# Batch 2's plain attention pairs computed in 64x64 quadrants, in three visits instead of two

## The chip, the cores and the metric

The kernel runs on one core of a Trainium2 chip. The metric is the device time of one execution in microseconds (us). The kernel before takes 300.69 us, the median of three runs (300.37 to 300.76). The engines are PE (TensorE, matrix multiply; PEld is its weight load), DVE (VectorE), ACT (ScalarE), POOL (GpSimd, which here mostly issues DMAs) and SP (SyncE, which issues DMAs). Each engine takes its own instructions strictly in the order in which the program wrote them, and waits on semaphores for the others.

## The reference

```
# q, k, v: 8 batches, 8 heads, 576 tokens, 64 dims; D = 64
mask_plain = (rel >= 0) & (rel < 32)                       # heads 0 to 3
mask_dil = (rel >= 0) & (rel < 128) & (rel % 4 == 0)       # heads 4 to 7
scores = where(mask, q @ k.T / sqrt(D), -1e9)
attn = exp(scores - max); attn /= sum(attn) + 1e-9
x = (attn @ v) reshaped to 4608 tokens x 512
h = maximum(x @ w_in, 0)                                   # 512 x 2048
out = (h * h) @ w_out                                      # 2048 x 512
```

So it is a banded attention, with half of the heads plain (the last 32 tokens) and half dilated (every fourth of the last 128), and then a two-layer network with a squared relu.

## The kernel before, in words

**The two layers set the pace.** The 4,608 tokens go through the layers in tiles: four of 256 tokens (they start at tokens 0, 256, 512, 768) and then seven of 512. A tile's work is cut into groups of a few matmuls, numbered from 0: first-layer groups (`mm1` in `ffn_groups`, line 905; the result goes through ACT's relu, L918, and DVE's square, L919) and second-layer groups (`g2`, line 947, four matmuls of 512 columns each; after four groups the output is copied to SBUF by ACT, L953, and stored by SP). The tile at token 768 has groups 48 to 63 (in order: 48 and 49 with the first three k-tiles, 50 and 51 with the last one, 52 to 55 whole, 56 to 63 second-layer); the tile at token 1024 starts at group 64. The tuple `kts` is the order in which a first-layer group takes its four k-tiles; k-tile e is the part of x that pair e of heads has written.

**Attention is put between the groups.** Heads go in pairs: pairs 0 and 1 are plain, 2 and 3 dilated. Work for a batch is a list of small steps, and a hand-written schedule says after which group each is emitted. There are two schedules: `PROGRAM`, a string whose parts between bars belong to groups -1, 0, 1, ..., and the list `steps` at the end of the kernel, of (group, rank within it, batch, code). Nothing reorders them later: the order of emission is the order on each engine.

A code of `PROGRAM` has batch, kind, pair and home: `2q1` and `2k1` turn pair 1's q and k of batch 2 by PE transposes (L258) and copy them from PSUM into `qT` (L278) and `kbd` (L282); who copies q follows `copier`: ACT for plain pairs, or DVE where the code ends in `v`. `2k1l` and `2k1h` do the two heads separately. `2a0` and `2b0` are the first and second part of pair 0's scores over the whole 128x128 array (L332), with ACT's exp (L342) and DVE's mask (L343). `2o0` and `2p0` are the products with v (L395) and the sums with ones (L397), with ACT's Ln and Exp (L399, L400) that make the reciprocal, and DVE's multiply into `xT` (L410). `1b3` and `1p3` are the same for batch 1. A pair's two heads share one 128-row operand there, with zeros in the other half (`kbd` and `vbd` hold block diagonals).

A code of `steps` that begins with V is a **visit**: the function `quadrants` takes scores of some pairs and products of others and issues them as 64x64 matmuls (L629), each on one of four quadrants of the array, which run side by side; the quadrant is (row half g, column half c). `V022,23/` is batch 2's scores of pairs 2 and 3. R00, R01, R10 and R11 (`arrange`, L479 and L482, on DVE) copy the end blocks of the dilated q and k for row half g (first digit) from the tile `xx` into `kbd`; a visit's dilated scores read both. E20 and E21 are the exp (ACT, L666) and mask (DVE, L668) of pair 2's two halves. L2 is the Ln of the sums (L642, L643), X2 the reciprocal's Exp (L652) and the multiply into `xT` (DVE, L655, L657). A plain pair in a visit also has two additions on DVE that its sums share (L680).

In the kernel before, batch 2 (`XB`) is mixed. Its dilated pairs go through visits: the scores after group 56, the products after group 59 together with batch 3's first scores (pair 2). Its plain pairs go through `PROGRAM`, over the whole array, between groups 39 and 56. Batches from 3 on are in quadrants throughout. The accumulators of a visit are PSUM tiles of four pools: `pa` (two buffers), `pf` (four), `po` and `pd` (one each); a visit waits until the buffers that it takes over have been read.

Of the kernel before, what the change touches and what calls it, by code (L numbers as in the profile page):

```python
# [12 lines left out]
RES = 4  # L13
# [12 lines left out]
    "X21 M21 L31 X31 M31 E01 E11 | L2:q00123 L2:q10123 L1:v1dpr | | P01 D01 L01 X01 M01 P11 D11 L11 X11 M11 | | | "  # L26
    "| | | | | | | | | m n | | | | | | 1q1 1q3 | 1q2f 1k2f | 1k1a 1v3 | 1a2 | 1v2 1k0a 1q0v | 1o2 | 1a0 1a1 | 1k3 "
    "1o0 1o1f | 1a3 1Q0 | 1K0 1o3 | 1Q1 1K1 | 1Q2 | 1b0 | | 1Q3 1K2 L2:vwp L3:q00123 L3:q10123 L2:vwdr | L2:x f | "
    "| 2q0 | | 2k0 1V2 | 1b2 1p0 | 1b1 1V3 1K3 | L3:x | 1p2 1p1f | 2a0 1b3 | 2k1l 2b0 2o0 1p3f 2k1h | 2q1 | | 2p0 "
    "L3:Vd0 L4:q00123 L4:q10123 L3:V1 2a1 | 2b1 | | 2o1 | | | 2p1f | | | | L4:x | | | | | | | | | | | | | | | | | "  # L30
    "| L4:Vd L5:q10123 L5:q00123 L4:V01 | | | | | | | | | | | | | | | | L5:x | L5:Vd L6:q10123 L6:q00123 L5:V01"
)


# [29 lines left out]
def kernel(  # L64
# [9 lines left out]
    nc = tc.nc  # L74
# [99 lines left out]

    def crossed(b: int, e: int):

        return int(b == XB and e == 3 or b >= NATURAL and e == 1 or b >= PAIRED and e == 0)

    def load_v(b: int, parts, which="pdr"):


        dst = vbd[b % 2]
        if b not in vds:
            vds[b] = vd_pool.tile([P, NE // 2, 2, RES * D], bf16, name="vd")
        p0, p1 = parts[0], parts[-1] + 1
        i0, i1 = 4 * p0, 4 if p1 == 1 else NB
        sides = [(hl, slice(64 * hl, 64 * hl + 64)) for hl in range(2)]
        for what in which:
            if what == "p":
                for e in range(NE // 2):  # L190
                    for hl, rows in sides:
                        nc.gpsimd.dma_start(  # L192
                            dst[rows, e, i0:i1, rows],
                            v[b, 2 * e + hl, 64 * i0 : 64 * i1, :].rearrange("(i p) d -> p i d", p=64),
                        )
            elif what == "d" and len(parts) == 1:
                for hl, rows in sides:
                    nc.gpsimd.dma_start(  # L198
                        vds[b][rows, :, p0, :],
                        v[b, H // 2 + hl : H : 2, 256 * p0 : 256 * p1, :].rearrange("e (p r) d -> p e (r d)", r=RES),  # L200
                    )
            elif what in "d01":
                for e in (0, 1) if what == "d" else (int(what),):
                    for hl, rows in sides[::-1] if crossed(b, e + NE // 2) else sides:
                        hl = hl ^ crossed(b, e + NE // 2)
                        nc.gpsimd.dma_start(
                            vds[b][rows, e, :, :],
                            v[b, H // 2 + 2 * e + hl, 0:512, :].rearrange("(m p r) d -> p m (r d)", p=64, r=RES),
                        )
            elif b == XB:  # L210
                for g, rows in sides:
                    for i in (0, 8):
                        nc.gpsimd.dma_start(
                            dst[rows, NE // 2 : NE, i, rows],
                            v[b, H // 2 + g : H - g : 3 - 2 * g, 64 * i : 64 * i + 64, :].rearrange("h p d -> p h d"),
                        )
            elif p1 == 2:
                for hl, rows in sides:
                    nc.gpsimd.dma_start(
                        dst[rows, NE // 2 : NE, 8, rows],  # L220
                        v[b, H // 2 + hl : H : 2, 512:S, :].rearrange("h p d -> p h d"),
                    )
# [271 lines left out]
    def quadrants(scs, pvs):  # L494
# [14 lines left out]
        for n, (b, e) in enumerate(pvs):  # L509
# [2 lines left out]
            o, d = (pool.tile([P, 512], f32, name=name) for pool, name in pools)  # L512
            if double:
                to = main_s[crossed(b, e)]
                rest = [to[:, 448:512]] * 2, [to[:, 384:448]] * 2
            else:
                rest = ([t[:, 448:512] for t in main_s],) * 2
# [64 lines left out]
        for n, (b, e) in enumerate(scs):  # L582
            ps = extra if n else main_s
            sp[b, e] = ps
            dil = e >= NE // 2
            swap = double and n == 0
            if swap:
                turned.add((b, e))
            for g, c in todo:
                items = scored[n][g, c]  # L590
                rows, h = sides[g], 2 * e + (c ^ crossed(b, e))
                to = ps[g ^ c if swap else g]
                for z in range(4):
                    if dil:
                        x, y = z % 2, 80 * z
                        lhs = kx[b % 2][rows, h, z // 2, 64 * x : 64 * x + 64]
                        rhs = qx[b % 2][rows, h, z // 2, 16 + 48 * x : 96 + 48 * x]
                        out, cols = to[:, y : y + 80], 80
                    else:
                        i = 2 * z + g  # L600
                        lhs, rhs = k_both[rows, i, h, :], q_both[rows, h, :, 16 * i : 16 * i + 24]
                        out, cols = byr(to[:, 96 * z : 96 * z + 96]), 96
                    items.append(("s", out[sides[c]], lhs, rhs, cols))
                if dil:
                    hd = h - H // 2
                    lhs, rhs, y = ends[b % 2][rows, 1, hd, :], byr(ends[b % 2][rows, 0, hd, :]), 320
                elif g == 0:
                    lhs, rhs, y = k_both[rows, 8, h, :], q_both[rows, h, :, 128:M], 384
                if dil or g == 0:
                    items.append(("s", byr(to[:, y : y + 64])[sides[c]], lhs, rhs, 64))  # L610
# [20 lines left out]
    def natural_step(b: int, code: str):  # L631
# [28 lines left out]
        else:  # L660
# [3 lines left out]
            n = 384 if e >= NE // 2 else (448, 384)[g]  # L664
            pt = pts[b, e][:, 448 * g : 448 * g + n]
            nc.scalar.activation(pt, sp[b, e][g][:, 0:n], ACT.Exp, scale=SCALE)  # L666
            mask = (mask_f if e >= NE // 2 else mask_n)[:, 0:n]
            nc.vector.tensor_tensor(out=pt, in0=pt, in1=mask, op=ALU.mult)  # L668
            if g and e >= NE // 2 and b > XB:
                z = pts[b, e][:, :].rearrange("p (x y) -> p x y", x=2)[:, :, 0:320].rearrange("p x (c m) -> p x c m", c=2)  # L670
# [206 lines left out]
    def ffn_groups(tk0: int, nt: int):  # L877
# [3 lines left out]
        early = NT <= tk0 <= 3 * NT  # L881
        h2 = h2_pool.tile([P, NF, NT], bf16, name="h2T")
        per = NT // nt
        kts = (2, 0, 3, 1) if tk0 > 3 * NT else (2, 3, 0, 1) if tk0 == 3 * NT else (0, 2, 1, 3) if NT <= tk0 < 2 * NT else (0, 1, 2, 3) if tk0 in (0, 2 * NT) else (2, 3, 0, 1)
        cut = 3 if tk0 >= NT and tk0 != 2 * NT else 2
        cur, acc = {}, {}

# [51 lines left out]
        def g2(m, part):  # L939
            last = tk0 + P * (m + 1) == NTOK  # L940
            if part == 0 or last and part == 2:
                cur[m] = ps_f.tile([P, DM], f32, name="pf")

            c0, c1 = ((0, 384), (384, DM))[part // 2] if last else (0, DM)
            f0, f1 = (NF // 2 * (part % 2), NF // 2 * (part % 2 + 1)) if last else (4 * part, 4 * part + 4)
            for f in range(f0, f1):
                nc.tensor.matmul(  # L947
                    cur[m][:, c0:c1], h2[:, f, P * m : P * m + P], w_out_sb[:, f, c0:c1],
                    start=(f == 0), stop=(f == NF - 1),
                )  # L950
            if f1 == NF:
                osb = osb_pool.tile([P, DM], f32, name="osb")
                (nc.vector.tensor_copy if last and part == 1 else nc.scalar.copy)(osb[:, c0:c1], cur[m][:, c0:c1])  # L953
                pos = tk0 + (P * m + half) % nt if over else tk0 + P * m
                for x in (c0, DM // 2) if c1 - c0 == DM and tk0 == NTOK - NT else (c0,):
                    store(osb, pos, x, DM // 2 if x < c0 + DM // 2 and c1 - c0 == DM and tk0 == NTOK - NT else c1)
# [123 lines left out]
    groups[:NF] = [head[y] for y in (0, 1, 2, 3, 16, 4, 5, 17, 18, 19, 20, 21, 6, 7, 22, 23)]  # L1080
    groups[NF:G] = [head[y] for y in (8, 9, 12, 13, 10, 11, 14, 15)] + head[24:32]
    for x, code in enumerate(("R00", "R01", "R10", "R11")):
        steps.append((48 + x, 1, XB, code))
    steps.append((56, 2, XB, "V022,23/"))
    steps += [(57, 1, XB, f"E{e}{x}") for e in (2, 3) for x in range(2)]
    for b in range(NATURAL, B):
        t = G * (b - 1)
        early = b == NATURAL
        def visit(at, scs, pvs):
            steps.append((at, 2, b, "V0" + "/".join(",".join(f"{x}{y}" for x, y in z) for z in (scs, pvs))))  # L1090

        def expo(e, *at):
            steps.extend((y, 1, b, f"E{e}{x}") for x, y in enumerate(at))
# [3 lines left out]

        after = b + 1 < B
        if b < PAIRED:
            start = 59 if early else t - 8  # L1100
            second = t + (7 if early else 5)
            x = 3 if early else 0
            if early:
                visit(start, [(b, 2)], [(XB, 2), (XB, 3)])
                for e in (2, 3):
                    steps.extend([(start + e - 2, 3, XB, f"L{e}"), (start + e - 1, 0, XB, f"X{e}")])
            expo(2, *((start + 4, start + 7) if early else (start + 7, start + 9)))
            visit(second, [(b, x)], [(b, 2)])
            norm(2, second)
            expo(x, second + 3, second + 5)  # L1110
# [81 lines left out]
```

## Time and profile before

| | |
|---|---|
| median of three runs | 300.69 us |
| the profiled execution | 300.98 us |
| its span, first to last instruction | 299.2 us |
| PE busy | 290.3 us, 97% |
| ACT busy | 195.2 us, 65% |
| DVE busy | 168.3 us, 56% |
| POOL busy | 129.4 us, 43% |

The profile is of one execution. Busy is the time in which at least one instruction of the engine ran. The span is cut into 40 slices of 7.5 us for the rows of digits, where 9 means 90% or more; the row PEclk is the granted TensorE clock in tenths. The chain of waits follows back from the last instruction to what released each, and gives shares of the span by engine. A timeline row has start, duration, engine, line, operation, output and inputs, shapes and a count; instructions overlap, so that the distance between starts tells more than the sum of durations.

Around the change, batch 2's work stands between 60 and 88 us: the first dilated scores begin at 80.57, the visit with the dilated products at 83.74, and the tile at token 1024 begins at 88.19.

### The profile page before, as it was taken

Reading aid. Unit: us, or ns where it says so; the run is one execution under the profiler, and the core shown is the slowest. Engines: PE = TensorE matmul, PEld = TensorE weight load, DVE = VectorE, ACT = ScalarE, POOL = GpSimd, SP = SyncE. Lnnn points to the kernel's source line nnn. Section 1 sums busy time; section 2 is a strip of 40 time slices with the busy share of each in tenths; the row PEclk is TensorE's granted clock in tenths of the full one; section 3 lists DMA queues with packets and bytes.
Section 4 is the critical chain, followed back from the end, with each engine's and each line's share of the span. In section 5 each row is a group of like instructions: output and inputs, shape, how many; then the busy total and the mean of one; then the engine's idle time right before and its main releaser. Section 6 shows DMA issues by size and latency. Waiting matters only on the chain.

```text
span 299.2 us, 7686 instructions
## 1 busy us (share of the span) xinstructions
PE 290.3 (97%) x3056; PEld 168.3 (56%) x3085; DVE 168.3 (56%) x503; ACT 195.2 (65%) x407; POOL 129.4 (43%) x210
## 2 busy tenths in 40 slices
PE   8989999999999999999999999999999999999994
PEld 3589756968855454554455455545554455445443
DVE  1676556997858764687749564866455234004300
ACT  6788658859967765788667666767666567127411
POOL 8589873484695475955792689000000000000000
PEclk9999999999999999999999999999999999999999
DMA  7999999999999989989999499012101200121022
GB/s 105 196 167 214 207 144 234 191 160 191 173 127 184 184 106 201 151 127 174 157 202 145 59 166 186 8 30 70 45 0 28 82 35 2 35 71 35 2 70 70
DMA packets 83123, 35.42 MB, mean 118 GB/s; under 512 B 52624, under 2 KB 78480, under 8 KB 83088
## 3 DMA queue, kind: packets, MB, share of 16 engines
q0 software_dynamic: 49280, 18.43, 54.7%
q1 hardware_dynamic: 33120, 16.18, 25.5%
q8 instruction: 24, 0.39, 0.5%
q10 hardware_dynamic: 688, 0.33, 0.5%
q14 instruction: 11, 0.09, 0.1%
HBM read 37.40 MB, written 9.44 MB: 157 GB/s over the span
## 4 chain that ended last, share of the span: by engine, by line
PE 89%; DMA 5%; POOL 3%; issue 1%; ACT 0%; DVE 0%; ACTq 0%; POOLq 0%
PE pf L947 41%; PE pf L905 40%; DMA w_in<-in_moe_w_in_dram 5%; PE po L629 2%; PE pa L258 1%; PE pa L629 1%; PE pf L629 1%; POOL vbd L192 1%; PE pd L629 1%; POOL qb L171 1%; POOL kb L171 1%; PE pa L332 1%; PE po L395 1%; PE pd L397 0%; POOL vd L198 0%
## 5 line engine op out<-in xcount | busy, mean ns | idle before, releaser
L905 PE MATMUL pf<-xT,w_in 128*128 128x512 bf16 (+1 forms) x697 | 128.2, 340 | 1.0 <-DMA w_in<-in_moe_w_in_dram 0.6
L947 PE MATMUL pf<-w_out_sb,h2T 128*128 128x512 bf16 (+2 forms) x570 | 127.4, 373 | 1.5 <-issue 0.6
L905 PEld LDWEIGHTS <-w_in 128*128 128x128 bf16 x704 | 77.8, 113 | 46.9 <-DMA w_in<-in_moe_w_in_dram 0.9
L918 ACT ACTIVATE h2T<-pf 128x512 bf16<-128x512 f32 x144 | 83.6, 599 | 30.0 <-PE pf L905 29.8
L919 DVE TENSOR_TENSOR h2T<-h2T 128x512 bf16<-128x512 bf16 x144 | 60.3, 425 | 60.2 <-ACT h2T L918 57.9
L947 PEld LDWEIGHTS <-h2T 128*128 128x128 bf16 x592 | 55.4, 98 | 61.2
L953 ACT COPY osb<-pf 128x512 f32<-128x512 f32 (+1 forms) x36 | 20.7, 575 | 51.1 <-PE pf L947 47.1
L457 POOL DMA_DIRECT2D vbd<-in_v_dram x80 | 43.4, 552 | 20.8 <-DMA kb<-in_k_dram 8.1
L171 POOL DMA_DIRECT2D qb<-in_q_dram x18 | 13.0, 720 | 12.8 <-DMA xx<-qb 9.2
L652 ACT ACTIVATE rec<-rec 128x576 f32<-128x576 f32 x22 | 15.0, 682 | 0.6
L192 POOL DMA_DIRECT2D vbd<-in_v_dram x16 | 10.9, 688 | 9.5 <-DMA kb<-in_k_dram 2.6
L666 ACT ACTIVATE pt<-pa 128x384 bf16<-128x384 f32 (+1 forms) x26 | 11.8, 495 | 4.5 <-DVE xT L657 2.7
L655 DVE TENSOR_TENSOR xT<-po,rec 128x512 bf16<-128x512 f32 x13 | 9.0, 692 | 8.8 <-ACT rec L652 8.5
L444 POOL DMA_DIRECT2D vd<-in_v_dram x20 | 12.1, 617 | 3.7 <-DMA vbd<-in_v_dram 2.0
L171 POOL DMA_DIRECT2D kb<-in_k_dram x18 | 12.7, 705 | 0.3 <-issue 0.2
L449 POOL DMA_DIRECT2D vbd<-in_v_dram x20 | 12.2, 631 | 0.9 <-DMA vbd<-in_v_dram 0.7
L668 DVE TENSOR_TENSOR pt<-pt,mask_n 128x448 bf16<-128x448 bf16 (+1 forms) x20 | 7.1, 373 | 9.4 <-ACT pt L666 9.3
L668 DVE TENSOR_TENSOR pt<-pt,mask_f 128x384 bf16<-128x384 bf16 x24 | 8.3, 355 | 5.8 <-ACT pt L666 5.8
L471 DVE COPY qT<-xx 64x576 bf16<-64x576 bf16 (+1 forms) x30 | 10.7, 358 | 0.6
L655 DVE TENSOR_TENSOR xT<-pf,rec 128x512 bf16<-128x512 f32 x9 | 6.2, 692 | 7.1 <-ACT rec L652 7.1
L629 PEld LDWEIGHTS <-vbd 64*64 64x64 bf16 x248 | 6.8, 107 | 3.8 <-issue 3.3
L473 DVE COPY kbd<-xx 64x320 bf16<-64x320 bf16 (+3 forms) x32 | 8.2, 256 | 0.6
(140 smaller groups left out, 323.2 us busy)
## 6 DMA issues: line engine op xcount, KB each, us to landing
qb<-in_q_dram POOLq DMA_DIRECT2D x7, 320.0 KB, 7.1
kb<-in_k_dram POOLq DMA_DIRECT2D x7, 320.0 KB, 8.1
vd<-in_v_dram POOLq DMA_DIRECT2D x32, 64.0 KB, 6.1
w_in<-in_moe_w_in_dram POOLq DMA_DIRECT2D x4, 512.0 KB, 7.7
w_out_sb<-in_moe_w_out_dram POOLq DMA_DIRECT2D x4, 512.0 KB, 12.7
out_dram<-osb SPq DMA_DIRECT2D x16, 128.0 KB, 4.3
qb<-in_q_dram POOLq DMA_DIRECT2D x7, 256.0 KB, 7.4
kb<-in_k_dram POOLq DMA_DIRECT2D x7, 256.0 KB, 7.6
```

The source lines that it names most:

```text
L171: nc.gpsimd.dma_start(t[0:n, part, hs, :], src[b, hs, t0 : t0 + RES * n, :].rearrange("h (p r) d -> p h (r d)", r=RES))
L192: nc.gpsimd.dma_start(dst[rows, e, i0:i1, rows], v[b, 2 * e + hl, 64 * i0 : 64 * i1, :].rearrange("(i p) d -> p i d", p=64),)
L457: nc.gpsimd.dma_start(v_rows[b % 2][p0 + 16 * r : p0 + 16 * r + 16, e, :, :], v[b, 2 * e + hl, :, :].rearrange("(i m r) d -> r m i d", r=R ...
L629: nc.tensor.matmul(out, lhs, rhs, start=begin, stop=True, skip_group_check=True)
L652: nc.scalar.activation(rec[:, :], rec[:, :], ACT.Exp, scale=-1.0)
L655: nc.vector.tensor_tensor(out=tok[:, :, 16:M], in0=byr(o[:, :]), in1=byr(rec[:, 0:512]), op=ALU.mult)
L668: nc.vector.tensor_tensor(out=pt, in0=pt, in1=mask, op=ALU.mult)
L905: nc.tensor.matmul(to, w_in_sb[piece][:, kt, c0 : c0 + 509 : 4], rhs, start=(kt == kts[0] and x == 0), stop=(kt == kts[-1] and x == per - ...
L918: nc.scalar.activation(hv, acc[u][:, :].rearrange("p (x n) -> p x n", x=per), ACT.Relu)
L919: nc.vector.tensor_tensor(out=hv, in0=hv, in1=hv, op=ALU.mult)
L947: nc.tensor.matmul(cur[m][:, c0:c1], h2[:, f, P * m : P * m + P], w_out_sb[:, f, c0:c1], start=(f == 0), stop=(f == NF - 1),)
L953: (nc.vector.tensor_copy if last and part == 1 else nc.scalar.copy)(osb[:, c0:c1], cur[m][:, c0:c1])
```

## The change

Batch 2's plain pairs go through visits too.

- `PROGRAM` loses 2a0, 2b0, 2o0, 2p0 and 2a1, 2b1, 2o1, 2p1. 2q1 becomes 2q1v: DVE copies the q of pair 1 instead of ACT.
- The visit with the dilated scores moves from after group 56 to after group 50; R00 to R11 go from groups 48, 49, 50, 51 to 48, 49, 49, 50. A second visit after group 55 has the plain scores and the dilated products. A third, after group 61 (it was after 59), has the plain products and batch 3's first scores.
- `quadrants` learns batch 2's plain scores: each head's nine blocks lie in one quadrant, pair 0 on (0,0) and (1,1), pair 1 on (0,1) and (1,0). For that, pair 1 is `crossed`: its v blocks are loaded with the two heads in the opposite halves.
- The mask of these pairs is a part of `mask_p` instead of `mask_n`. The spare columns for the end blocks come from another tile where a visit has two of each kind.
- The tile at token 1024 takes its k-tiles in the order 2, 3, 0, 1 instead of 0, 1, 2, 3. The two output copies of the tile at token 768 go from ACT to DVE.

```diff
-    "| 2q0 | | 2k0 1V2 | 1b2 1p0 | 1b1 1V3 1K3 | L3:x | 1p2 1p1f | 2a0 1b3 | 2k1l 2b0 2o0 1p3f 2k1h | 2q1 | | 2p0 "
-    "L3:Vd0 L4:q00123 L4:q10123 L3:V1 2a1 | 2b1 | | 2o1 | | | 2p1f | | | | L4:x | | | | | | | | | | | | | | | | | "
+    "| 2q0 | | 2k0 1V2 | 1b2 1p0 | 1b1 1V3 1K3 | L3:x | 1p2 1p1f | 1b3 | 2k1l 1p3f 2k1h | 2q1v | | L3:Vd0 "
+    "L4:q00123 L4:q10123 L3:V1 | | | | | | | | | | L4:x | | | | | | | | | | | | | | | | | | L4:Vd L5:q10123 "
...
-        return int(b == XB and e == 3 or b >= NATURAL and e == 1 or b >= PAIRED and e == 0)
+        return int(b == XB and e in (1, 3) or b >= NATURAL and e == 1 or b >= PAIRED and e == 0)
...
-                            v[b, 2 * e + hl, 64 * i0 : 64 * i1, :].rearrange("(i p) d -> p i d", p=64),
+                            v[b, 2 * e + (hl ^ crossed(b, e)), 64 * i0 : 64 * i1, :].rearrange("(i p) d -> p i d", p=64),
...
                 to = main_s[crossed(b, e)]
+                if full and scs[0][1] < NE // 2:
+                    to = (extra if n else main_s)[1]
...
-            swap = double and n == 0
+            swap = double and n == 0 and dil
...
+                if b == XB and not dil:
+                    for i in range(NB) if c == g ^ crossed(b, e) else ():
+                        z, y = 96 if i < 8 else 64, 96 * (i // 2)
+                        out = byr(ps[i % 2][sides[c], y : y + z])
+                        rows = sides[g]
+                        items.append(
+                            ("s", out, kbd[rows, e, i, rows], qT[rows, e, :, 16 * i : 16 * i + z // RES], z)
+                        )
+                    continue
...
-            mask = (mask_f if e >= NE // 2 else mask_n)[:, 0:n]
+            mask = (mask_f if e >= NE // 2 else mask_p[:, 384:] if b == XB else mask_n)[:, 0:n]
...
-        kts = (2, 0, 3, 1) if tk0 > 3 * NT else (2, 3, 0, 1) if tk0 == 3 * NT else (0, 2, 1, 3) if NT <= tk0 < 2 * NT else (0, 1, 2, 3) if tk0 in (0, 2 * NT) else (2, 3, 0, 1)
+        kts = (2, 0, 3, 1) if tk0 > 3 * NT else (2, 3, 0, 1) if tk0 in (2 * NT, 3 * NT) else (0, 2, 1, 3) if NT <= tk0 < 2 * NT else (0, 1, 2, 3) if tk0 == 0 else (2, 3, 0, 1)
...
-                (nc.vector.tensor_copy if last and part == 1 else nc.scalar.copy)(osb[:, c0:c1], cur[m][:, c0:c1])
+                (nc.vector.tensor_copy if last and part == 1 or tk0 == 3 * NT // 2 else nc.scalar.copy)(osb[:, c0:c1], cur[m][:, c0:c1])
...
-        steps.append((48 + x, 1, XB, code))
-    steps.append((56, 2, XB, "V022,23/"))
-    steps += [(57, 1, XB, f"E{e}{x}") for e in (2, 3) for x in range(2)]
+        steps.append(((48, 49, 49, 50)[x], 1, XB, code))
+    steps.append((50, 2, XB, "V022,23/"))
+    steps += [(50 + e - 2 + x, 3, XB, f"E{e}{x}") for e in (2, 3) for x in range(2)]
+    steps.append((55, 2, XB, "V020,21/22,23"))
+    steps += [(55, 3, XB, "E10"), (55, 3, XB, "E11"), (55, 3, XB, "L3"), (56, 0, XB, "X3")]
+    steps += [(56, 1, XB, "E00"), (56, 1, XB, "E01"), (57, 3, XB, "L2"), (58, 0, XB, "X2")]
...
-            start = 59 if early else t - 8
+            start = 61 if early else t - 8
...
-                visit(start, [(b, 2)], [(XB, 2), (XB, 3)])
-                for e in (2, 3):
-                    steps.extend([(start + e - 2, 3, XB, f"L{e}"), (start + e - 1, 0, XB, f"X{e}")])
-            expo(2, *((start + 4, start + 7) if early else (start + 7, start + 9)))
+                visit(start, [(b, 2)], [(XB, 0), (XB, 1)])
+                for y, e in enumerate((1, 0)):
+                    steps.extend([(start + y, 3, XB, f"L{e}"), (start + y + 1, 0, XB, f"X{e}")])
+            expo(2, *((start + 3, start + 6) if early else (start + 7, start + 9)))
```

Lines of the changed kernel are 11 higher than those named here from about line 660 to 1080.

## The prediction

> **What bounds the kernel now.** I read the page first: its busy table and its chain of waits.
>
> ```profile
> PE 290.3 (97%) x3056; PEld 168.3 (56%) x3085; DVE 168.3 (56%) x503; ACT 195.2 (65%) x407; POOL 129.4 (43%) x210
> ...
> PEclk9999999999999999999999999999999999999999
> ...
> PE 89%; DMA 5%; POOL 3%; issue 1%; ACT 0%; DVE 0%; ACTq 0%; POOLq 0%
> ```
>
> TensorE (PE) is busy 97% of the span, at full granted clock, and holds 89% of the chain; DVE and ACT hold 0%. After the first weights land (24.5 us) PE never rests for long. So the sum is simple: the end moves by the PE time that is taken out, plus every new wait that PE takes on.
>
> Next I read PE's timeline where batch 2's plain pairs stand now. Columns: start, us, engine, line, operation, tiles, shape, count. The time of a piece is the distance to the start of the next piece (the second column has the pipeline's tail in it).
>
> ```profile
> 68.11 0.32 PE L332 MATMUL pa<-qT,kbd 128*128 128x96 bf16 x4
> 68.27 0.41 PE L338 MATMUL pa<-qT,kbd 128*128 128x32 bf16 x8
> ...
> 69.69 0.39 PE L332 MATMUL pa<-qT,kbd 128*128 128x32 bf16 x6
> 69.92 0.32 PE L395 MATMUL po<-pt,vbd 128*128 128x96 bf16 x4
> 70.07 0.32 PE L397 MATMUL pd<-pt,mk 128*128 128x96 bf16 x4
> 70.23 0.44 PE L395 MATMUL pf<-pt,vbd 128*128 128x32 bf16 x9
> ...
> 72.04 0.45 PE L258 MATMUL pa<-mk,qb 80*128 80x80 bf16 x8
> 72.32 1.91 PE L905 MATMUL pf<-xT,w_in 128*128 128x256 bf16 x16
> 74.08 0.39 PE L395 MATMUL po<-pt,vbd 128*128 128x32 bf16 x6
> 74.30 0.39 PE L397 MATMUL pd<-pt,mk 128*128 128x32 bf16 x6
> 74.52 0.32 PE L332 MATMUL pa<-qT,kbd 128*128 128x96 bf16 x4
> ```
>
> Pair 0's pieces are scores 0.16 (68.11) and 0.23 (69.69), products 0.31 (69.92 to 70.23) and 0.44 (74.08 to 74.52): 1.14 us; the two pairs 2.28.
>
> Last I read DVE's timeline, because the visit that the change pulls forward lives on what DVE writes.
>
> ```profile
> 69.98 0.98 DVE L282 COPY kbd<-pa 64x288 bf16<-64x288 bf16 x2
> ...
> 73.81 0.19 DVE L479 COPY kbd<-xx 64x128 bf16<-64x128 bf16 x1
> 73.92 0.30 DVE L482 COPY kbd<-xx 64x128 bf16<-64x128 bf16 x1
> 74.23 0.19 DVE L479 COPY kbd<-xx 64x128 bf16<-64x128 bf16 x1
> ...
> 78.44 0.19 DVE L479 COPY kbd<-xx 64x128 bf16<-64x128 bf16 x1
> ```
>
> L479 with L482 is one step R (end blocks of q and k): 0.42 us. The fourth, R11, runs at 78.44; the visit that reads it begins at 80.57. Today it has 2 us to spare.
>
> **PE work, part by part.** Out: the plain pieces, 2.28, and the two old visits, 0.70 (80.57 to the next GEMM at 81.27) and 1.21 (83.74 to 84.95): 4.19. In: three visits. Group 50's (dilated scores) holds the same 40 matmuls as the old one: 0.70. Group 55's has per quadrant 1,536 columns of dilated products and 832 of plain scores, 2,368; the nearest row is the visit of 108 matmuls and up to 2,272 columns at 141.45 to 142.64, 1.19, which scaled by columns is 1.24. Group 61's has 1,440 columns of plain products and 384 of batch 3's scores, 1,824, the same form as the visit at 111.61 to 112.83: 1.22. Together 3.16. **Net -1.03 us**. Taken alone that would be the gain.
>
> **What loses its cover.** I take the before trace's clock up to 68.11 and follow the built order of the changed kernel, with durations of these rows.
>
> PE: 1b3's scores 68.11 to 68.39, four GEMMs (0.86) to 69.25, the k transposes to 69.54. The products 1p3 come next, with no 2b0 and 2o0 in between. They need 1b3's mask: ACT's previous Exp ends 68.77, the exp of 512 (0.59) about 69.3, DVE's mask (0.43) 69.76. PE waits 0.26, and does the products (0.49) until 70.29. Then 12 GEMMs (1.31), q transposes (0.29), 12 GEMMs (1.31), 4 GEMMs (0.44): at **73.64** PE arrives at group 50's visit. Some 320 columns in, at 73.8, its last end blocks need R11.
>
> DVE, strictly in its order: two L282 after the mask, 0.98, to 70.7; the L410 multiply of 1p3, whose Ln and Exp put it 1.17 us behind the sums (66.80 to 67.97 in an earlier step), at 71.46 to 71.87; two more L282 to 72.9; then the four copies of 2q1, which ACT did until now; R00, R01, R10, 1.26; two squares L919 (0.76 for two), which stand ahead of R11; R11, 0.42.
>
> The four q copies (64x288, from PSUM, on DVE) are not in the trace. Below: the same line on DVE at 64x160 (58.31 to 59.34, four in 1.03) gives 1.03. Above: L282 at 64x288, about 0.49 each, 1.96. I take 1.30, 0.325 each, from the growth of that line from 64x128 (222 ns) to 64x160 (239 ns). So R11 ends at 72.9 + 1.30 + 1.26 + 0.76 + 0.42 = 76.6. PE is released at about 76.7: **a new wait of 2.9 us**, in three pieces (PSUM buffer of the q copies, R01, R11). Queued behind it on PE is everything: the GEMMs, whose relus feed ACT.
>
> [...]
>
> Even a faster DVE leaves a floor. The squares wait for two relus of the last four GEMMs: the first starts about 73.6, the two take 1.08 (ACT's pair at 74.16), a square 0.42, R11 0.42: 75.5. The wait is at least 1.7.
>
> Behind it things are tight but nearly covered. Between the visits of groups 55 and 61 stand 24 GEMMs, 5.2 us; ACT has exps, logarithms and reciprocals of 4.6 and DVE a multiply of 0.9 behind them, overlapping by some 0.5: 0 to 0.3 of wait. After group 61's visit PE has eight GEMMs, then eight with the k-tiles 2 and 3 that the new order puts first, 3.46 us; the last multiply of today's visit ends 3.35 after the visit (88.29 against 84.95). I put 0.2 on both; without the new k-tile order it would be 1.7 more.
>
> At nothing: exp, mask, sums and normalisation of the plain pairs (ACT gives up 5.4 us and takes 5.1; DVE gives up 3.3 and takes 4.1, some 0.8 more) run under GEMMs. The two output copies moved from ACT (0.58 each) to DVE aren't shown in that shape; DVE's 128x384 copy is 0.56 and its 128x512 multiply from PSUM 0.69, so I take 0.69. Both run under the GEMMs between visits 55 and 64; if that cover went, the last multiply, and PE, would be up to 0.7 late. The v loads swap halves, with as many DMAs; SP's and POOL's orders stay. The q and k transposes that group 50 reads landed by 62.2, the dilated v of group 55 by 77.9, before either is wanted.
>
> **Sum.** -1.03 + 0.26 + 2.9 + 0.2 - 0.1 (a wait before the visit at 80.57 that goes) = +2.2 us. The profiled run took 300.98 (span 299.2, 1.8 around it), 0.29 above the median 300.69; on the median this is **302.9**.
>
> **Rivals.**
> 1. *The visit does not wait* (faster): if R11 were done when PE comes, at 73.8, -1.03 + 0.26 - 0.1 = -0.9 stays, 299.8. For it: DVE is busy only 56%, and R has 2 us of slack today. Against: the visit moves from 80.57 to 73.64, 6.9 us forward, and R11 with it only by as much as DVE's queue lets it; R11 would have to end 2.8 us sooner, and it stands behind squares that PE's own last GEMMs release. The change is a gain where this wait stays below 0.7 (0.9 less the 0.2 at the later visits). Chance 0.10.
> 2. *DVE is quicker than I think, ACT's relus set the wait*: the floor, 1.7, with no waits later: +0.6 to +1.4, 301.3 to 302.1. For it: DVE is idle 0.7 before the multiply at 71.46. Chance 0.16.
> 3. *More is late*: copies at 0.49 (+0.7), 0.5 more at groups 55, 61 and 64, together 304.1; I give it 303.7 to 304.6. Chance 0.12. PEclk is 9 throughout today, so no row shows what a PE that stands for 2.9 us does to the granted clock. [...]
> 4. *The quadrants bring less*: if the plain pairs' two diagonals did not run side by side, the visits at 55 and 61 cost the 832 + 1,440 columns again, 0.95, and the gain goes: about 303.9, in case 3's range. Against it: the 111.61 row, the same form. Chance 0.03.
> The forecast, 302.1 to 303.7, keeps 0.59.
>
> **Numbers.** A measurement of this kernel tells about 0.2% (0.6 us) from no change. Faster by more: 0.10. Within: 0.05 (the low end of case 2, and a wait of about 1). Slower: 0.85. The range is 301.2 to 304.2: the forecast, most of case 2 and the near part of case 3.
>
> **What would show it.** Right: in the changed trace PE's visit of 40 matmuls, near 73.6, lasts about 3.4 us rather than 0.70, its weight load waiting for DVE L482, while DVE shows no gap from 71.5 to 76.6; the visits at 55 and 61 take about 1.24 and 1.22. Wrong: that visit in under 1.5 us; q copies on DVE far from 0.31; or a long wait at the first GEMMs on tokens 1024 and up.

## The result, and the profile after

The changed kernel takes 304.88 us (median; 304.21 to 306.36) beside 301.06 us of the kernel before in the same sessions: a ratio of 1.0135, 95% interval 1.0107 to 1.0163, or 4.1 us more. The forecast was 302.9 and its range ended at 304.2: the direction was right, the size too small. The profiled execution took 305.68 us, with a span of 303.8.

The page of the changed kernel, the same three rows as before:

```profile
PE 294.6 (97%) x3129; PEld 168.2 (55%) x3129; DVE 171.2 (56%) x513; ACT 192.7 (63%) x399; POOL 129.1 (42%) x210
...
PEclk9999999999799999999999999999999999999999
...
PE 89%; DMA 5%; DVE 2%; POOL 1%; ACT 1%; issue 1%; ACTq 0%; POOLq 0%
```

Two things are new. DVE has 2% of the chain, where it had 0%, and the clock row has a 7. PE's busy share is still 97%, so the busy table shows neither: a PE at half clock counts as busy (3.41 of 3.41 us in the stretch at 0.50 below).

PE's timeline, where the visit of group 50 now stands (L640 is a visit's matmul, L916 a GEMM, that is a matmul of the two layers, here of the first; the bracket is idle time and who ended it):

```profile
73.80 0.22 PE L640 MATMUL pa<-xx 64*64 64x80 bf16 x2
74.40 0.33 PE L640 MATMUL pa<-xx 64*64 64x80 bf16 x14 [0.38 <-DVE qT L278]
75.46 0.22 PE L640 MATMUL pa<-kbd 64*64 64x64 bf16 x2 [0.73 <-DVE kbd L482]
77.26 0.22 PE L640 MATMUL pa<-kbd 64*64 64x64 bf16 x2 [1.58 <-DVE kbd L482]
...
77.58 5.79 PE L916 MATMUL pf<-xT,w_in 128*128 128x256 bf16 x36
```

The visit begins at 73.80 and the next GEMM at 77.58: 3.78 us for 40 matmuls that take 0.48 in e1 below, where nothing holds them up, so 3.30 of waiting, in the three pieces that were forecast. (The brackets add up to 2.69; they leave out the tail of the matmul ahead of each wait.) The last row is what was not forecast: 36 GEMMs take 5.72 us until the next visit, at 83.30. In the kernels below that have no clock dip here they take 4.05 or 4.06.

DVE in the same stretch (L278 are the q copies, L479 and L482 the steps R, L930 the squares):

```profile
72.05 1.00 DVE L282 COPY kbd<-pa 64x288 bf16<-64x288 bf16 x2
73.08 1.26 DVE L278 COPY qT<-pa 64x288 bf16<-64x288 bf16 x4
74.38 0.32 DVE L479 COPY kbd<-xx 64x128 bf16<-64x128 bf16 x1
...
75.55 0.46 DVE L482 COPY kbd<-xx 64x128 bf16<-64x128 bf16 x1
76.02 0.76 DVE L930 TENSOR_TENSOR h2T<-h2T 128x512 bf16<-128x512 bf16 x2
76.79 0.19 DVE L479 COPY kbd<-xx 64x128 bf16<-64x128 bf16 x1
76.90 0.30 DVE L482 COPY kbd<-xx 64x128 bf16<-64x128 bf16 x1
```

DVE works without a gap from 71.53 until R11 is done at 77.2, and PE follows at 77.26. It is a queue of 5.7 us on an engine that is busy 56% of the span.

Last the busy time by stretches, cut where the clock record changes (columns: length, then busy time with instructions of PE, PEld, DVE, ACT, POOL; granted clock; DMA share; GB/s):

```profile
71.61:75.03 3.42, 2.74 (x43) 2.29 (x40) 3.24 (x11) 1.09 (x2) 2.72 (x5) 1.00 1.42 181
75.03:78.44 3.41, 1.40 (x32) 1.25 (x33) 2.47 (x9) 0.90 (x2) 1.59 (x4) 1.00 1.85 143
78.44:81.85 3.41, 3.41 (x18) 2.44 (x17) 2.27 (x6) 2.84 (x7) 3.41 (x7) 0.50 1.49 248
81.85:85.26 3.41, 3.41 (x118) 2.77 (x117) 2.40 (x8) 2.40 (x6) 3.41 (x7) 1.00 0.75 71
```

The granted clock is exactly 0.50 from 78.44 to 81.85, 3.41 us, and 1.00 on both sides. In the 3.41 us ahead of the dip PE was busy 1.40 us, 41%. The slow GEMMs cost 5.72 - 4.05 = **1.67 us**. Five of the six executions have a mean clock of 0.992 to 0.994, as this one; the sixth, the fastest (304.21), has 0.997 and left no trace.

### The profile page after: what moved, and what is told of

Read it like the earlier page. It is cut to its first block, busy times and chain, and to the rows that moved or that the text cites. A ratio compares the mean times of both kernels' runs of the same rounds, so it can differ in the third digit from the quotient of the medians.

```text
span 303.8 us, 7800 instructions
## 1 busy us (share of the span) xinstructions
PE 294.6 (97%) x3129; PEld 168.2 (55%) x3129; DVE 171.2 (56%) x513; ACT 192.7 (63%) x399; POOL 129.1 (42%) x210
## 4 chain that ended last, share of the span: by engine, by line
PE 89%; DMA 5%; DVE 2%; POOL 1%; ACT 1%; issue 1%; ACTq 0%; POOLq 0%
PE pf L958 41%; PE pf L916 40%; DMA kb<-in_k_dram 3%; DMA w_in<-in_moe_w_in_dram 2%; PE po L640 2%; PE pf L640 1%; PE pa L640 1%; PE pa L258 1%; PE pd L640 1%; POOL qb L171 1%; ACT rec L399 0%; POOL kb L171 0%; DVE qT L278 0%; DVE kbd L482 0%; POOL vbd L219 0%
## 5 line engine op out<-in xcount | busy, mean ns | idle before, releaser
L916 PE MATMUL pf<-xT,w_in 128*128 128x512 bf16 (+1 forms) x704 | 130.3, 344 | 0.7 <-DMA w_in<-in_moe_w_in_dram 0.5
L958 PE MATMUL pf<-w_out_sb,h2T 128*128 128x512 bf16 (+2 forms) x592 | 129.5, 373 | 0.0
L916 PEld LDWEIGHTS <-w_in 128*128 128x128 bf16 x704 | 78.6, 114 | 48.4 <-issue 0.8
L930 DVE TENSOR_TENSOR h2T<-h2T 128x512 bf16<-128x512 bf16 x144 | 60.2, 425 | 61.6 <-ACT h2T L929 59.5
L964 ACT COPY osb<-pf 128x512 f32<-128x512 f32 (+1 forms) x34 | 19.5, 574 | 49.6 <-PE pf L958 46.6
L677 ACT ACTIVATE pt<-pa 128x384 bf16<-128x384 f32 (+1 forms) x28 | 12.8, 498 | 6.3 <-DVE xT L668 3.6
L663 ACT ACTIVATE rec<-rec 128x576 f32<-128x576 f32 x24 | 16.4, 682 | 0.7
L666 DVE TENSOR_TENSOR xT<-po,rec 128x512 bf16<-128x512 f32 x14 | 9.7, 691 | 7.4 <-ACT rec L663 6.9
L666 DVE TENSOR_TENSOR xT<-pf,rec 128x512 bf16<-128x512 f32 x10 | 6.9, 692 | 9.0 <-ACT rec L663 9.0
L640 PEld LDWEIGHTS <-vbd 64*64 64x64 bf16 x288 | 7.6, 107 | 4.2 <-issue 2.5
L677 ACT ACTIVATE pt<-pf 128x448 bf16<-128x448 f32 (+1 forms) x18 | 8.5, 520 | 0.5 <-PE pf L640 0.3
```

Source lines behind the costliest of these rows:

```text
L640: nc.tensor.matmul(out, lhs, rhs, start=begin, stop=True, skip_group_check=True)
L663: nc.scalar.activation(rec[:, :], rec[:, :], ACT.Exp, scale=-1.0)
L666: nc.vector.tensor_tensor(out=tok[:, :, 16:M], in0=byr(o[:, :]), in1=byr(rec[:, 0:512]), op=ALU.mult)
L916: nc.tensor.matmul(to, w_in_sb[piece][:, kt, c0 : c0 + 509 : 4], rhs, start=(kt == kts[0] and x == 0), stop=(kt == kts[-1] and x == per - ...
L930: nc.vector.tensor_tensor(out=hv, in0=hv, in1=hv, op=ALU.mult)
L958: nc.tensor.matmul(cur[m][:, c0:c1], h2[:, f, P * m : P * m + P], w_out_sb[:, f, c0:c1], start=(f == 0), stop=(f == NF - 1),)
```

## The experiments

**Theory**: the loss is PE's wait for DVE in group 50's visit (3.3; the expectations say 3.1, which takes 0.70 for the visit itself) and a clock dip that this wait causes (1.7); without both, most of the forecast's net gain on PE (1.0) is left. **Rival 1**: the dip comes from the visits' denser work, not from standing. **Rival 2**: DVE's queue is not what delays the visit, its new place is. All times are relative to the kernel before in the same session; the wait is the length of group 50's visit less 0.48; "dip" is a half clock between 70 and 95 us in the profiled execution.

| run | ratio to before, 95% interval | wait in group 50's visit, us | dip |
|---|---|---|---|
| changed kernel | 1.0135 (1.0107 to 1.0163) | 3.30 | yes |
| e1 | 1.0008 (0.9992 to 1.0024) | 0 | no |
| e2 | 1.0059 (1.0035 to 1.0083) | 1.86 | no |
| e3 | 1.0035 (1.0015 to 1.0056) | 1.23 | no |
| e4 | 1.0107 (1.0073 to 1.0141) | 0.66 | no |
| e5 | 1.0202 (1.0170 to 1.0234) | 0 | yes, behind 90.6 |
| e6 | 1.0055 (1.0036 to 1.0074) | 0 | no |
| e7 | 1.0025 (1.0008 to 1.0042) | 0 | no |
| e8 | 1.0105 (1.0070 to 1.0139) | 2.32 | no |
| e9 | 1.0004 (0.9988 to 1.0019) | 0 | no |
| e10 | 0.9988 (0.9972 to 1.0005) | 0 | no |
| e11 | 1.0183 (1.0161 to 1.0205) | 4.63 | yes, twice as long |
| e12 | 1.0124 (1.0104 to 1.0143) | 0.22 | no |
| e13 | 0.9988 (0.9970 to 1.0005) | 0 | no |

**e1: both causes of the wait taken away.**

```diff
-    ... | 2k1l 1p3f 2k1h | 2q1v | ...
+    ... | 2k1l 1p3f 2k1h | 2q1 | ...
-        steps.append(((48, 49, 49, 50)[x], 1, XB, code))
+        steps.append(((44, 46, 46, 47)[x], 1, XB, code))
```

> The changed kernel with two edits: ACT copies pair 1's q again, and R00, R01, R10, R11 are emitted after groups 44, 46, 46, 47 (instead of 48, 49, 49, 50), ahead of the q copies and the squares in DVE's queue. Theory (the loss is PE's wait of about 3.1 us in group 50's visit for DVE, and 1.8 us more because the granted clock goes to 0.5 for 3.4 us behind it): that visit lasts 0.7 to 1.0 us instead of 3.8, the granted clock stays 1.0, ACT is some 0.8 late at group 55; in all 1.0 faster to 0.1 slower than the kernel before. Rival 1 (the dip of the clock comes from the denser work of the visits, not from PE's standing): the visit is short, yet the clock dips as in the changed kernel, about 1.4 slower than before. Rival 2 (DVE's queue is not what delays the visit; moving it to group 50 is): at least 2 slower than before.

PE's timeline of e1:

```profile
74.02 4.12 PE L916 MATMUL pf<-xT,w_in 128*128 128x256 bf16 x36
...
78.07 0.22 PE L640 MATMUL po<-pt,vd 64*64 64x80 bf16 x1
78.72 0.21 PE L640 MATMUL po<-pt,vbd 64*64 64x64 bf16 x1 [0.42 <-DMA vbd<-in_v_dram]
```

The visit of group 50 takes 0.48, the clock stays 1.0, the 36 GEMMs take 4.05: rivals 1 and 2 fall. All of the loss is gone, but nothing is gained. The next rows say where it went: the visit of group 55 now comes at 78.07, and the last v blocks that it multiplies land at 78.68. It takes 1.88 instead of 1.26.

**e2 and e3: each edit alone.** e2 has only the first line of e1's diff, e3 only the second.

> The changed kernel with one edit: ACT copies pair 1's q again. Theory: R11 still stands behind two squares, PE waits about 1.75 us for it in group 50's visit, in one piece. If a wait of that length leaves the clock at 1.0: about 1.3 slower than before; if the clock dips as in the changed kernel: about 3.1 slower. Rival 1 (the dip is from the visits' work): it dips, 3.1. Rival 2 (not DVE's queue): about 4 slower, as the changed kernel.

> The changed kernel with one edit: R00, R01, R10, R11 after groups 44, 46, 46, 47; the q copies stay on DVE. Theory: PE waits about 1.1 us in group 50's visit for the PSUM buffer of the q copies, the clock stays 1.0: about 0.6 slower than before. Rival 1 (the dip is from the visits' work): about 2.4 slower. Rival 2 (not DVE's queue): about 4 slower.

PE's timeline of e2, and a row of its busy times by stretches:

```profile
76.19 0.22 PE L640 MATMUL pa<-kbd 64*64 64x64 bf16 x2 [1.62 <-DVE kbd L482]
76.51 4.12 PE L916 MATMUL pf<-xT,w_in 128*128 128x256 bf16 x36
```

```profile
74.32:77.73 3.41, 1.78 (x51) 1.63 (x45) 2.19 (x8) 2.09 (x5) 2.76 (x6) 1.00 1.37 177
```

PE's timeline of e3:

```profile
75.01 0.33 PE L640 MATMUL pa<-xx 64*64 64x80 bf16 x14 [1.02 <-DVE qT L278]
75.47 4.12 PE L916 MATMUL pf<-xT,w_in 128*128 128x256 bf16 x36
...
87.03 0.22 PE L640 MATMUL po<-pt,vbd 64*64 64x96 bf16 x2 [0.85 <-DVE xT L666]
```

The waits, 1.86 and 1.23, came close to what was expected (1.75 and 1.1), and neither dips. The stretch of e2 that holds its wait is busy 1.78 of 3.41, 52%, and the clock stays. In time e2 lost 1.8 (1.3 expected) and e3 1.1 (0.6 expected). What e3 has beyond that wait stands in its last row: group 61's visit waits for a DVE multiply. DVE's timeline of e3 has the reason:

```profile
85.43 0.19 DVE L479 COPY kbd<-xx 64x128 bf16<-64x128 bf16 x1 [0.88 <-DMA xx<-qb]
...
86.29 0.69 DVE L666 TENSOR_TENSOR xT<-po,rec 128x512 bf16<-128x512 f32 x1
```

DVE stands 0.88 us at batch 3's R00, until the DMA of its q lets it start at 85.43, and the multiply that PE wants is queued behind it.

**e4: PE works while it waits.** The changed kernel, with this ahead of the visit of group 50:

```diff
+            to = ps_o.tile([P, 512], f32, name="po")
+            for _ in range(12):
+                nc.tensor.matmul(
+                    to[:, :], mask_d[:, 0:P], mask_d[:, 256:768], start=True, stop=True, skip_group_check=True
+                )
```

> The changed kernel with 12 more matmuls on PE ahead of group 50's visit (128x128 by 512 columns each, on constants, into a PSUM buffer that nobody reads; 0.216 us each at full clock, 2.6 in all), so that PE works while it would wait for DVE. Theory: the visit still ends when R11 comes, at about 77.3 to 77.6, but the clock stays 1.0 behind it: 1.8 faster than the changed kernel, about 2.2 slower than before. Rival 1 (the dip is from the visits' work or density): the clock dips all the same, time as the changed kernel, about 4 slower than before, or more.

PE's timeline of e4 (L674 are the added matmuls, L922 the first-layer GEMMs):

```profile
73.45 2.75 PE L674 MATMUL po<-mask_d 128*128 128x512 bf16 x12
...
76.95 0.22 PE L640 MATMUL pa<-kbd 64*64 64x64 bf16 x2 [0.46 <-DVE kbd L482]
77.27 4.12 PE L922 MATMUL pf<-xT,w_in 128*128 128x256 bf16 x36
```

The visit ends within 0.3 us of when it did, yet there is no dip, and the profiled execution is 1.82 shorter than the changed kernel's (303.86 against 305.68). But the median, 304.53, is only 0.4 below: of its four executions two took 305.2 and 305.3 at a mean clock of 0.996 and 0.993. They left no trace, so where they were slow isn't shown. e11 and e12 ask the question again without that doubt.

**e5: v ahead of batch 3's second half of q and k** (in e1's kernel, after which all that follow are edits of e1).

```diff
-    ... L2:vwp L3:q00123 L3:q10123 L2:vwdr | ...
+    ... L2:vwp L3:q00123 L2:vwdr L3:q10123 | ...
```

> e1's kernel with batch 2's dilated v loads (12 DMAs on POOL, their last four landed at 78.68 in e1, after the visit of group 55 had begun at 78.07) put ahead of the second half of batch 3's q and k loads. Theory (what keeps e1 from its gain of about 0.8 is this landing, 0.62): they land before 78, that visit takes 1.26 instead of 1.88, and the kernel is 0.4 to 0.7 faster than before. Rival: the loads that are pushed back (q and k of batch 3, whose transposed second halves landed at 82.8 in e1) make DVE's R00 of batch 3 late, which stands ahead of the multiplies, and the visit of group 61 waits instead: no gain, or up to 1 slower than before.

```profile
90.62 0.26 PE L640 MATMUL po<-pt,vbd 64*64 64x96 bf16 x2 [4.46 <-DVE xT L666]
```

The rival holds, by far more than it expected. Group 55's visit (79.29 to 80.81) no longer waits for v, but PE's timeline (above) shows group 61's visit waiting 4.46 us for DVE's multiply. That DVE stands at R00 there, for a later q than in e3, is the rival's reading. A clock dip follows the wait: from 90.84 on the visit's products of 96 columns into `po` start 0.07 to 0.08 us apart, where in e1 it is 0.04 to 0.05, and the execution's mean clock is 0.993. In both orders that were tried one of these visits waits: 0.42 for the DMA of v in e1, 4.46 here.

**e6: the old order of k-tiles; e7: the output copies back on ACT.**

```diff
-        kts = ... (2, 3, 0, 1) if tk0 in (2 * NT, 3 * NT) ... (0, 1, 2, 3) if tk0 == 0 ...
+        kts = ... (2, 3, 0, 1) if tk0 == 3 * NT ... (0, 1, 2, 3) if tk0 in (0, 2 * NT) ...
```

```diff
-                (nc.vector.tensor_copy if last and part == 1 or tk0 == 3 * NT // 2 else nc.scalar.copy)(...)
+                (nc.vector.tensor_copy if last and part == 1 else nc.scalar.copy)(...)
```

> e1's kernel with the tile at token 1024 taking its k-tiles in the old order 0, 1, 2, 3. The prediction says that this costs 1.7: theory, 1.7 slower than e1, as a wait of the second or third GEMM of that tile for the multiply into k-tile 0. Rival (ACT and DVE have these multiplies done in time): as e1.

> e1's kernel with the two output copies of the tile at token 768 back on ACT. Theory (a copy ahead of the logarithms of group 61's visit costs its own 0.58 there, less what stood idle): 0.3 to 0.5 slower than e1, as a longer wait at the tile at token 1024. Rival (ACT has the time): as e1.

PE's timeline at the tile of token 1024, e6 and then e7:

```profile
89.59 1.24 PE L916 MATMUL pf<-xT,w_in 128*128 128x512 bf16 x5 [1.72 <-DVE xT L668]
```

```profile
91.09 0.59 PE L916 MATMUL pf<-xT,w_in 128*128 128x512 bf16 x2 [0.39 <-DVE xT L668]
```

Both waits are there, 1.72 and 0.39, and by the ratios the kernels are 1.4 and 0.5 slower than e1. The new k-tile order earns its place. For the copies the evidence is thinner: e7's interval overlaps e1's, and its trace has another wait, 0.67 in group 61's visit.

**e8: a wait and nothing else.**

```diff
+    steps += [(47, 1, XB, "R11")] * 7
```

> e1's kernel with the step R11 done seven more times on DVE ahead of group 50's visit (0.42 each, 2.9 in all; they write the same values again), so that the visit waits about 2.7 us in one piece, with no other cause of the changed kernel. Theory (a PE that stands so long has the granted clock halved for the next 3.4 us): a dip to 0.5 behind the visit in most executions, mean clock 0.994; the wait of 2.7 swallows e1's 0.6 at group 55; 3.5 to 3.9 slower than e1. Rival 1 (the dip is not from standing): clock 1.0, 2.0 to 2.2 slower than e1.

The wait was 2.11 by its bracket (2.7 expected), and the profiled execution has no dip. In the changed kernel's trace the clock changes at 78.44, at 81.85 (3.41 later) and again at 303.72 (221.87 later, 65 stretches of 3.413), so the busy times are cut on such a grid. For e8 its place is an estimate: 67 of these stretches behind 72.00 is 300.67, and a half clock from there to the end of the span, 301.1, gives the mean clock measured, 0.999. Two of its rows:

```profile
72.00:75.41 3.41, 2.05 (x35) 1.74 (x32) 3.27 (x16) 3.04 (x7) 2.48 (x5) 1.00 1.49 177
75.41:78.83 3.42, 2.67 (x44) 2.62 (x45) 2.89 (x12) 1.89 (x5) 1.69 (x3) 1.00 2.34 73
```

The wait fell across two stretches, which are still busy 60% and 78%. Of the four executions two took 302.74 and 303.19 (clock 1.0 and 0.999), two 304.35 and 305.99 (0.994 and 0.992). So the expectation "in most executions" was too strong. By an estimate the place of the grid may decide (a wait of 2.11 within one stretch of 3.41 would leave it busy 38% at most), but the two with the lower clock left no trace. Inconclusive by itself, which is why e11 waits longer.

**e11 and e12: a longer wait, and the same wait filled.** e11 has 12 instead of 7 in e8's line. e12 adds e4's matmuls to it, 20 of them.

> e8's kernel with the step R11 done twelve more times instead of seven, so that group 50's visit waits about 4.2 us in one piece. Theory (a wait of this length leaves a stretch of 3.4 us in which PE works less than half the time, wherever it falls): the granted clock is 0.5 for 3.4 us in every execution, mean clock at most 0.995; 2.1 us of wait and 1.7 of slow clock more than e8 without a dip: about 5.8 slower than before. Rival (standing does not cost clock): 1.0, about 4.2 slower than before.

> e11's kernel with 20 matmuls on constants (128x128 by 512 columns, 0.216 us each, 4.3 in all) on PE ahead of the visit, which fill the wait. Theory: the visit ends when it does in e11, the clock stays 1.0, 1.7 faster than e11 although PE has more to do, about 4.1 slower than before. Rival: as e11, or slower by what the 20 matmuls add.

PE's timeline of e11, then of e12:

```profile
78.08 0.26 PE L640 MATMUL pa<-kbd 64*64 64x64 bf16 x2 [4.23 <-DVE kbd L482]
78.59 6.52 PE L916 MATMUL pf<-xT,w_in 128*128 128x256 bf16 x36
```

```profile
73.92 4.26 PE L674 MATMUL po<-mask_d 128*128 128x512 bf16 x19
...
78.81 4.12 PE L922 MATMUL pf<-xT,w_in 128*128 128x256 bf16 x36
```

This is the plainest pair. The visit ends at 78.6 and 78.8. Behind it the same 36 GEMMs take 6.45 us (to 85.04) and 4.05 (to 82.86). The medians are 306.68 and 304.96: **more work on PE makes the kernel 1.72 us faster**, as the theory said (1.7). All executions of e11 have a mean clock of 0.992 or less, all of e12 of 0.997 or more. The stretches of e11:

```profile
73.33:76.75 3.42, 0.51 (x21) 0.24 (x18) 3.33 (x19) 1.59 (x4) 2.85 (x5) 1.00 1.62 152
76.75:80.16 3.41, 2.08 (x30) 1.58 (x31) 2.56 (x11) 0.92 (x2) 1.76 (x4) 0.50 1.26 177
80.16:83.57 3.41, 3.41 (x18) 2.43 (x17) 1.98 (x6) 2.40 (x6) 3.35 (x7) 0.50 1.20 178
```

The dip was expected to last 3.4 us and lasts two stretches: PE stands in the first part of the second one too. So the agreement of 1.72 with 1.7 is partly luck: the theory priced one stretch, and in the traces two of them cost 6.45 - 4.05 = 2.40 us, while the executions of e11 spread from 305.80 to 307.31.

**e9, e10, e13: where e1's gain goes.** In group 55's visit, e9 issues the end blocks' matmuls last in every quadrant; e10 also emits batch 3's R00 and R01 after group 58 instead of 57; e13 is e10 with another order.

```diff
+        if full and scs[0][1] < NE // 2:
+            for items in todo.values():
+                items.sort(key=lambda x: x[0] != "s" and x[4] == 64)
```

```diff
-            steps.append(((57, 57, 54, 55)[x] if early else at + x, 1, b, code))
+            steps.append(((58, 58, 54, 55)[x] if early else at + x, 1, b, code))
```

```diff
-            for items in todo.values():
-                items.sort(key=lambda x: x[0] != "s" and x[4] == 64)
+            for g in range(2):
+                todo[g, g].sort(key=lambda x: 2 * (x[0] == "s") or x[4] == 64)
```

> e1's kernel, with the matmuls of the end blocks in group 55's visit (64 columns each; those that read the v that landed at 78.68 in e1) issued as the last of their quadrants instead of, on row half 1, as the first. Theory (e1's gain goes into the wait for this landing, 0.4 to 0.7): the wait is hidden behind about 1 us of other matmuls of the visit, which takes 1.3 instead of 1.9, and the kernel is 0.5 to 0.7 faster than before. Rival (batch 3's q and k, which landed at 82.8, and DVE's queue behind them set the time of group 61's visit): that visit waits for what group 55's saves, and the time is as e1's, within 0.2 of before.

> e9's kernel, with R00 and R01 of batch 3 emitted after group 58 instead of 57, behind the multiplies of group 55's second pair, so that a late landing of batch 3's q and k holds up only the last scores of group 61's visit and not the multiplies that free its PSUM buffers. Theory (in e3 and e7 that visit waited 0.85 and 0.67 for DVE's multiply, which stood behind R00 and R01): 0 to 0.3 faster than e9, and less spread. Rival (R00 and R01 are then themselves too late): 0.2 to 0.6 slower than e9.

> e10's kernel with another order in group 55's visit: only in the two quadrants (0,0) and (1,1), whose first products read the late v, the 64-column matmuls of the end blocks go behind the other products and sums and ahead of the scores; the other two quadrants keep the order of e1. Theory (e10's visit takes 1.59 only because of its order, and the landings no longer hold anything up): the visit takes 1.25 to 1.35, 0.2 to 0.35 faster than e10, 0.4 to 0.7 faster than before. Rival (the landing of batch 3's q and k sets group 61's visit in any order): the 0.3 comes back as a wait there or at the tile at token 1024, and the time is as e10's, within 0.2 of 0.3 faster than before.

The wait for v is gone in all three, but group 55's visit takes 1.59, 1.59 and 1.52, not 1.3. In e9 group 61's visit waits 0.92 for DVE's multiply behind R00, as in e3: the rival. In e10 it doesn't wait, and e10 is 0.5 faster than e9 by the ratios, with intervals that overlap. e13 is no better than e10, so the order of the matmuls was not what made the visit long. PE's timeline of e13 inside that visit, and ACT's before it (L932 are the relus):

```profile
78.26 0.19 PE L643 MATMUL pf<-qT,kbd 64*64 64x64 bf16 x1
78.42 0.19 PE L643 MATMUL pf<-pt,vd 64*64 64x80 bf16 x1
...
78.76 0.20 PE L643 MATMUL pf<-pt,vd 64*64 64x80 bf16 x1
78.92 0.23 PE L643 MATMUL pf<-pt,mk 64*64 64x160 bf16 x2
```

```profile
77.19 1.68 ACT L932 ACTIVATE h2T<-pf 128x512 bf16<-128x512 f32 x3
```

The visit wants four `pf` buffers. The second of the three relus ends at 78.37 and the next `pf` matmul starts at 78.42; the third ends at 78.86 and the next starts at 78.92. ACT runs without a gap from 71.7 to 79.3 there. The match in time is what speaks for it; no run took the relus away.

The best median, e13's 300.37 beside 300.93, has an interval from 0.9970 to 1.0005: no version beats the kernel before beyond doubt.

## Why the prediction was wrong

| term | predicted | measured in the traces |
|---|---|---|
| PE's work | -1.03 | -0.98 |
| mask of 1b3 | +0.26 | +0.23 |
| wait in group 50's visit | +2.9 | +3.30 |
| clock behind it | 0 | **+1.67** |
| first GEMMs at token 1024 | +0.2 with the visits | +0.15 (7.15 against 7.00) |
| wait ahead of a visit | -0.1 | +0.10 |
| sum | +2.2 | +4.47 |

The last term: PE takes about 0.1 more ahead of each of these visits (24 GEMMs of 0.216, as eight take 1.73 at 102.94 in the trace before, take 5.27 ahead of group 61's), and there are now three instead of two. The sum can be checked between two points that both traces have, the GEMMs ahead of 1b3's scores (67.25 before, 67.35 after) and the visit inside the tile at token 1024 (95.19 and 99.76): 32.41 - 27.94 = 4.47. The ratio of all executions says +4.1 (3.2 to 4.9); the traced one was 0.8 above its median.

**Right in its sum, wrong in its parts: PE's work.** The trace of the kernel before lacks some matmul records. Its page has 3,056 on PE beside 3,085 weight loads; the changed kernel's has 3,129 of both. Behind both old visits the first GEMM is missing:

```profile
80.57 0.34 PE L629 MATMUL pa<-xx 64*64 64x80 bf16 x16
...
81.27 2.54 PE L947 MATMUL pf<-w_out_sb,h2T 128*128 128x512 bf16 x11 [0.16 <-issue]
...
84.95 3.40 PE L947 MATMUL pf<-w_out_sb,h2T 128*128 128x512 bf16 x15 [0.16 <-issue]
```

Three groups of four give 11 records and four groups 15, and PE is idle for no reason that the profile shows. So "the next GEMM" there is the second, and the visits took 0.48 and 1.00 instead of 0.70 and 1.21; the model for group 61's visit, at 111.61, is 1.00 instead of 1.22 for the same reason. Out are then 3.76, in are 0.48, 1.26 and 1.04, 2.78. The same error stood on both sides, and -1.03 came out nearly right by luck.

**Right: the wait, its place and its cause.** PE comes at 73.80 (73.64 predicted), the q copies take 1.26 (1.30), R11 ends at 77.2 (76.6). The 0.6 is R00, R01 and R10 at 1.64 instead of 1.26 and a somewhat later start; less the 0.16 by which PE comes later, it makes the wait 0.40 longer than predicted. e1 to e3 show that this queue is the cause.

**Left out of the sum: the granted clock.** Rival 3 says that "no row shows what a PE that stands for 2.9 us does to the granted clock", and the sum has nothing for it; the 1.67 is most of what the sum lacks. In the traces no wholly idle stretch was needed: 41% busy was followed by the dip in the changed kernel, while 52% in e2 and 60% in e8 were not. e11 and e12 show that standing is the cause: with the same queue on DVE, the 36 GEMMs behind a wait of 4.23 take 6.45 us, and 4.05 where matmuls fill it. e5 has the longest wait in one piece, 4.46, and a dip behind it. e8's low mean clocks, 0.994 and 0.992, come in two of four executions; what decides that isn't shown.

**Wrong: rival 1's price, "-0.9 stays, 299.8".** e1 is the case that it describes, with no wait, and it equals the kernel before. Its trace shows where the 0.98 goes: 0.23 to the mask, 0.62 to group 55's visit, 0.16 to the tile at token 1024, 0.10 to the third visit's start. The prediction held that the v of group 55 lands "before either is wanted". That was true only of a PE that had stood 3 us. A PE that comes on time finds three other bounds close behind one another: v (0.62 in e1), DVE's multiplies behind batch 3's late q (0.85 in e3, 0.92 in e9) and, by the match in time alone, ACT's relus (about 0.26).

**Right: the k-tile order.** "Without the new k-tile order it would be 1.7 more": e6 waits 1.72. The output copies were put at nothing, as running under the GEMMs; in the changed kernel the tile behind them is 0.15 longer, and no run tests the "up to 0.7 late" of copies on DVE that lose this cover. e7 has them on ACT and waits 0.39.

**Open.** How much of the 0.98 would show if the DMAs came earlier: e5 only moved the lateness. What the executions of e4 that left no trace did. Where between 41% and 52% the clock turns, and whether that share is what decides.

## What to carry to other kernels

A stall of PE has a second price: count PE's busy share in the 3.41 us around it, and where that can fall to what dipped here (41%; 52% did not), allow for a half clock behind it (1.67 us in the changed kernel, 2.40 in e11), or fill the stall with work. Before a step is pulled forward, list when every operand of the steps behind it lands: slack is measured against the old time of use, and a step that comes 5 us sooner uses it up. A saving on the bounding engine is worth only the distance to the next bound, here nothing.

## What was not expected of the hardware

A kernel can be faster with more matmuls: 20 useless ones, 4.3 us of PE time, made e12 1.72 us faster than e11. The clock has only two values in the records of the kernels before and after and in the stretches of e11, 1.0 and 0.5, and a dip lasts whole stretches of 3.41 us (3.41 in the changed kernel, 6.83 in e11). In e11 the second stretch shows PE busy 2.08 of 3.41, 61%, and a second dip follows; at half clock that is, by an estimate, the work of 30% at full clock. That looks as if the work done counted and not the time busy, beside the 41% at full clock that a dip followed in the changed kernel; but one case doesn't settle it. The L482 copies took 0.36 to 0.46 us at 74.5 to 76.0 and 0.30 later. POOL was issuing DMAs at 74.5 to 76.0, but also at 83.73, where a copy took 0.30, so that alone doesn't explain it; what slows them was not tried.
